# A fused attention and FFN kernel: stores split by token parity, matmuls without a reader among the first units, and PSUM copies and loads reordered

## The chip, the cores and the metric

The kernel runs on one core of a Trainium2 chip. The metric is the device time of one execution in microseconds (us). A "fast" run is one at most 1.5% above the fastest of the same kernel; all comparisons below are between fast runs. The span in a profile is 1.8 to 1.9 us shorter than the measured time of the same execution, because it reaches from the first to the last instruction only.

## The reference

```python
# attention with decay, in blocks of 64 tokens; q, k, v are (4, 8, 768, 64), lam is (8,)
for b in range(nb):
    intra = (q_b @ k_b.T * Dmask) @ v_b
    inter = (q_b * lam_pow) @ kv_state
    out_b = intra + inter
    kv_state = lam_block * kv_state + (k_b * rev_pow).T @ v_b
x = out.transpose(0, 2, 1, 3).reshape(3072, 512)
# FFN: w_in is 512 x 2048, w_out is 2048 x 512
h = x @ w_in
g = h + sin(alpha * h)**2 / alpha
return g @ w_out                      # (3072, 512), float32
```

## The kernel before

In this kernel TensorE does the matrix products ("matmuls") and writes them to the buffer PSUM; the other tiles lie in the buffer SBUF; inputs and outputs lie in HBM, the main memory. In the listings `QT` is a transposed copy of q or k, `okv` the output of a unit in PSUM, `xt` its copy in SBUF, `hps` the result of the first FFN product and `ob` an output block; a "step" of the unit loop is the time from one unit to the next.

The work is cut into 24 attention units (four of them make 512 tokens, a "group") and into FFN steps. The order in time is: units 0 to 7 (two groups); then FFN steps alone, 16 of group 0 (`hook0`) and 8 of group 1 (`hook1`); then "macros", in which a unit, FFN steps and a block of the last matrix product are woven together; then the last four output blocks.

The parts that matter here:

```python
# one 128-token output block: PSUM -> SBUF -> HBM
nc.scalar.copy(out=ob[:], in_=ops[:])
nc.sync.dma_start(out=out[r0:r0 + C, :].rearrange("(p two) d -> two p d", two=2),
                  in_=ob[:])

# one FFN step: four matmuls into hps, then
s1 = sin(alpha * hps)          # ScalarE, reads PSUM
s2 = s1 * s1                   # VectorE, GpSimd or ScalarE, by a list
gall = s2 * r + hps            # VectorE, reads PSUM and SBUF

# one of the first eight units, n
scale_q(n + 1, V); scale_k(n + 1, G)
okv = new_okv()                       # one PSUM buffer, so it waits for its last reader
intermm(n - 1, okv); outmm(n - 1, okv)
scores(n); domask(n)
kvmm(n, okv); kv_copy(n, okv); kv_decay(n, 0)
transposes(n + 1, tag, True)          # eight on TensorE, then the QT copies
outev(n - 1, okv)                     # the xt copy: last reader of okv; ScalarE
cast_v(n + 1, A)
# ... (cut)
SQ = (V, A, G, G)                     # engines of the squares, used in turn
def hook0(f):
    # ... (cut: decays, load_w_out every fourth step)
    if f == GATE:
        load(8, after=f1mm[0, f]); load(9); load(10); load(11)
def hook1(f):
    if f == 1: scale(8, G, G, A)
    if f == 3: transposes(8, "s0"); scale(9, G, G, A)
alone(NFC, hook0, (V, A, V, G))       # 16 steps of group 0
alone(NPRE, hook1)                    # 8 steps of group 1, with SQ
```

V is VectorE, A is ScalarE, G is GpSimd.

## Time and profile before

253.46 us, the median of three runs (252.28 to 255.07); the profiled execution took 254.61 us.

| stretch of the profile | us | what bounds it |
|---|---|---|
| 0 to 37.50 | 37.5 | units 0 to 7: a loop over TensorE and ScalarE, with TensorE at half clock (sixteen score matmuls take 0.64 us, later 0.42) |
| 37.50 to 73.14 | 35.6 | FFN steps alone, then the first macro |
| 73.14 to 237.96 | 164.8 | macros and last blocks: TensorE, over 97% busy |
| 237.96 to 252.83 | 14.9 | no engine works |

First the end. This is the table of busy time by stretch for the kernel before: the stretch in us from the start, its length, each engine's busy us and instructions, the granted TensorE clock, the mean busy share of the 16 DMA engines, and GB/s.

```profile
223.00:238.00 15.00, 13.92 (x63) 6.17 (x63) 0.75 (x1) 2.61 (x5) 0.00 (x0) 1.00 0.13 45
238.00:242.00 4.00, 0.00 (x0) 0.00 (x0) 0.00 (x0) 0.00 (x0) 0.00 (x0) 0.80 0.13 51
242.00:247.00 5.00, 0.00 (x0) 0.00 (x0) 0.00 (x0) 0.00 (x0) 0.00 (x0) 0.50 0.13 51
```

From 238 us on every engine's column is zero, and the DMA share stands at 0.13. That is not a lightly loaded DMA: the share is a mean over 16 engines, and 2 of them fully busy make 0.125. The trace's packet records agree: from 242 to 250 us exactly two packets are under way at any moment. Each store raises its semaphore three times, once 0.93 to 1.15 us after the issue and twice when the data land (7.71 and 7.90 us after it for the store of 216.38 us, which did not queue). So stores of 256 KB go at 51 GB/s, 5.1 us each, while the last blocks are finished every 3.45 us. A queue of stores builds up, and the kernel ends when it has drained.

Now the loop of the first units, in the timeline of the kernel before (start in us, duration in us, engine, source line, operation, count, and in brackets the idle time before and what ended it). L294 are the inter-chunk matmuls, L215 the score matmuls, L193 the transposes, L197 the QT copy, L320 the xt copy.

```profile
22.18 0.37 PE L294 MATMUL okv<-QT,kvbd_495 128*128 128x128 bf16 x2 [0.99 <-ACT xt L320]
22.48 0.64 PE L309 MATMUL okv<-ST,VB 64*64 64x128 bf16 x16
22.91 0.64 PE L215 MATMUL sp<-QT 64*64 64x128 bf16 x16
23.34 0.42 PE L243 MATMUL okv<-VB,KD 64*64 64x64 bf16 x16
...
24.10 0.63 PE L193 MATMUL pt<-iden,KD 128*128 128x128 bf16 x4
...
24.81 0.59 ACT L197 COPY QT<-pt 128x512 bf16<-128x512 bf16 x1 [0.62 <-PE pt L193]
...
25.30 0.59 ACT L320 CAST xt<-okv 128x512 bf16<-128x512 f32 x1
...
25.94 0.37 PE L294 MATMUL okv<-QT,kvbd_581 128*128 128x128 bf16 x2 [1.21 <-ACT xt L320]
```

A unit takes 25.94 - 22.18 = 3.76 us. Its last link is the xt copy, which ScalarE starts only after the QT copy, which waits for the transposes; then TensorE has idled for 1.21 us.

The clock of TensorE can't be read from the page here. Its clock row shows full speed for this stretch, but the durations do not: sixteen score matmuls take 0.64 us here and 0.42 us after 65 us. It is plainest in the weight loads of the first FFN matmuls (PEld; one precedes each matmul of 512 columns):

```profile
37.93 0.15 PEld L338 LDWEIGHTS <-w_in_sb 128*128 128x128 bf16 x1 [0.28 <-issue]
38.35 0.15 PEld L338 LDWEIGHTS <-w_in_sb 128*128 128x128 bf16 x1 [0.28 <-issue]
38.78 0.15 PEld L338 LDWEIGHTS <-w_in_sb 128*128 128x128 bf16 x1 [0.27 <-issue]
```

They come every 0.427 us, twice the 0.216 us of later ones. The trace's first clock record of this run is of 42.4 us, 4.9 us after the first FFN matmul, and the spacing halves there; before the first record the row has nothing to show and prints full speed.

### The profile page before, as it was taken

To read this page: it belongs to the slowest core of one execution; us is meant where nothing else is said; L and a number is where in the kernel's file an instruction comes from. 1 tells how busy PE (TensorE), PEld (TensorE's weight loads), DVE (VectorE), ACT (ScalarE), POOL (GpSimd) and SP (SyncE) were. 2 spreads that over 40 slices of the span, in tenths; PEclk is the share of its full clock that TensorE was granted. 3 is DMA by queue.
4 is the path that set the end of the run, shared out by engine and by line. 5 is a ranking of instruction groups with operands and counts; after the bars stand their busy time and mean duration, and the time that the engine had idled before them with its cause. 6 is when DMAs were issued, how large, how long until landed. Compare 5 with 4: busy or idle time off the path is not lost.

```text
span 252.8 us, 5265 instructions
## 1 busy us (share of the span) xinstructions
PE 213.1 (84%) x2106; PEld 113.7 (45%) x2129; DVE 152.4 (60%) x260; ACT 130.8 (52%) x214; POOL 118.5 (47%) x184
## 2 busy tenths in 40 slices
PE   0867759976899999999999999999999999989500
PEld 0546543433355554555455545454554444434200
DVE  3667534898576665686669666876686667630000
ACT  2454545967766665656565656565655444520100
POOL 5665861989569998855683366236110000000000
PEclk9999999999999999999999999999999999999955
DMA  6999596599944544444533453201010111111110
GB/s 165 292 287 256 85 157 100 99 250 225 286 108 150 161 132 150 148 130 124 155 113 104 133 155 113 83 32 41 25 30 34 40 33 36 37 38 51 51 51 37
DMA packets 45560, 29.71 MB, mean 117 GB/s; under 512 B 1488, under 2 KB 42464, under 8 KB 45536
## 3 DMA queue, kind: packets, MB, share of 16 engines
q1 hardware_dynamic: 41280, 25.17, 35.0%
q0 software_dynamic: 4224, 4.19, 10.6%
q8 instruction: 16, 0.26, 0.4%
q14 instruction: 8, 0.07, 0.1%
q10 hardware_dynamic: 32, 0.01, 0.0%
HBM read 27.28 MB, written 6.29 MB: 133 GB/s over the span
## 4 chain that ended last, share of the span: by engine, by line
PE 75%; ACT 6%; POOL 5%; DVE 3%; issue 3%; DMA 1%; ACTq 0%; POOLq 0%
PE ops L365 33%; PE hps L338 27%; PE pt L193 6%; PE sp L215 3%; PE okv L309 3%; PE okv L294 3%; ACT xt L320 2%; DVE gall L352 2%; ACT QT L197 2%; PE okv L243 1%; DMA lam_bc<-in_lam_dram 1%; POOL KD L166 1%; ACT ob L372 1%; POOL E L123 1%; POOL s_944 L351 1%
## 5 line engine op out<-in xcount | busy, mean ns | idle before, releaser
L338 PE MATMUL hps<-xt,w_in_sb 128*128 128x512 bf16 x364 | 96.1, 387 | 5.4 <-DVE gall L352 2.5
L365 PE MATMUL ops<-w_out_sb,gall 128*128 128x512 bf16 x381 | 94.6, 379 | 0.9 <-ACT ob L372 0.7
L338 PEld LDWEIGHTS <-w_in_sb 128*128 128x128 bf16 x384 | 36.8, 99 | 48.2 <-issue 9.0
L365 PEld LDWEIGHTS <-gall 128*128 128x128 bf16 x384 | 36.9, 98 | 42.6 <-issue 1.0
L226 DVE TENSOR_TENSOR ST<-sp,mask 128x512 bf16<-128x512 f32 x48 | 30.8, 684 | 10.4 <-PE sp L215 10.4
L166 POOL TENSOR_TENSOR KD<-st_k,R 128x512 bf16<-128x512 f32 x24 | 26.9, 1121 | 3.5 <-DMA st_k<-in_k_dram 3.0
L200 ACT COPY QT<-pt 128x1024 bf16<-128x1024 bf16 x16 | 16.2, 1012 | 22.8 <-PE pt L193 22.8
L372 ACT COPY ob<-ops 128x512 f32<-128x512 f32 x24 | 14.1, 586 | 19.1 <-PE ops L365 19.1
L193 PE MATMUL pt<-iden,QL 128*128 128x128 bf16 x96 | 11.1, 248 | 8.8 <-DVE QL L157 6.6
L320 ACT CAST xt<-okv 128x512 bf16<-128x512 f32 x24 | 14.1, 588 | 6.4 <-PE okv L243 5.1
L157 POOL TENSOR_TENSOR QL<-st_q,E 128x512 bf16<-128x512 f32 x16 | 17.4, 1088 | 0.0
L193 PEld LDWEIGHTS <-QL 128*128 128x128 bf16 x96 | 7.7, 109 | 13.3 <-DVE QL L157 6.6
L215 PE MATMUL sp<-QT 64*64 64x128 bf16 x384 | 11.8, 252 | 0.7 <-ACT QT L197 0.7
L309 PE MATMUL okv<-ST,VB 64*64 64x128 bf16 x384 | 11.4, 248 | 0.0
L193 PE MATMUL pt<-iden,KD 128*128 128x128 bf16 x96 | 11.2, 250 | 0.3 <-POOL KD L166 0.3
L175 ACT CAST VB<-st_v 128x512 bf16<-128x512 f32 x14 | 8.7, 621 | 4.8 <-DMA st_v<-in_v_dram 4.8
L215 PEld LDWEIGHTS <-QT 64*64 64x64 bf16 x384 | 8.0, 127 | 2.9 <-ACT QT L197 0.9
L309 PEld LDWEIGHTS <-VB 64*64 64x64 bf16 x384 | 7.7, 123 | 1.7 <-issue 1.6
L193 PEld LDWEIGHTS <-KD 128*128 128x128 bf16 x96 | 7.6, 113 | 1.0 <-POOL KD L166 1.0
L243 PE MATMUL okv<-VB,KD 64*64 64x64 bf16 x320 | 8.1, 212 | 0.0
L197 ACT COPY QT<-pt 128x512 bf16<-128x512 bf16 x8 | 4.7, 586 | 5.6 <-PE pt L193 5.6
L243 PEld LDWEIGHTS <-KD 64*64 64x64 bf16 x320 | 6.9, 130 | 0.0
(528 smaller groups left out, 307.0 us busy)
## 6 DMA issues: line engine op xcount, KB each, us to landing
st_q<-in_q_dram SPq DMA_DIRECT2D x24, 256.0 KB
st_k<-in_k_dram SPq DMA_DIRECT2D x24, 256.0 KB
st_v<-in_v_dram SPq DMA_DIRECT2D x24, 256.0 KB
out_dram<-ob SPq DMA_DIRECT2D x24, 256.0 KB
w_in_sb<-in_moe_w_in_dram POOLq DMA_DIRECT2D x4, 512.0 KB, 6.3
w_out_sb<-in_moe_w_out_dram POOLq DMA_DIRECT2D x4, 512.0 KB, 9.1
lam_bc<-in_lam_dram SPq DMA_DIRECT2D x1, 4.0 KB
alpha_r<-in_moe_alpha_dram ACTq DMA_DIRECT2D x1, 8.0 KB
```

The source lines that it names most:

```text
L157: eng.tensor_tensor(out=QL[:], in0=stage[u][0][:].rearrange("p h two e -> p two h e"), in1=E[:, :, hs].unsqueeze(3).to_broadcast([P, 2, HH ...
L166: eng.tensor_tensor(out=KD[:], in0=stage[u][1][:].rearrange("p h two e -> p two h e"), in1=R[:, :, hs].unsqueeze(3).to_broadcast([P, 2, HH ...
L193: nc.tensor.transpose(out=pts[j][:, hp, par, :], in_=cast[u, key][:, par, 2 * hp:2 * hp + 2, :], identity=iden[:])
L200: nc.scalar.copy(out=QT[:], in_=pt[:])
L215: nc.tensor.matmul(out=sp[hd][half[c], par, hp, :], lhsT=QT[half[hd], 1, hp, par, half[c]], rhs=QT[half[hd], 0, hp, :, half[c]], start=Tru ...
L226: nc.vector.tensor_tensor(out=ST[:, hd], in0=sp[hd][:], in1=mask[:].unsqueeze(2).to_broadcast([P, 2, 2, P]), op=ALU.mult)
L243: nc.tensor.matmul(out=okv[half[hd], c, 2 * P + hp * D:2 * P + (hp + 1) * D], lhsT=KD[half[c], par, h, :], rhs=VB[half[c], par, h, :], sta ...
L309: nc.tensor.matmul(out=okv[half[hd], c, hp * P:(hp + 1) * P], lhsT=VB[half[c], par, 2 * hp + hd, :], rhs=ST[half[c], hd, par, hp, :], star ...
L320: nc.scalar.copy(out=xt[g][:, 2 * hh:2 * hh + 2, bb, :, :].rearrange("p hp c i -> p c hp i"), in_=okv[:, :, 0:2 * P].rearrange("p c (hp i) ...
L338: f1mm[g, f] = nc.tensor.matmul(out=hps, lhsT=w_in_sb[:, c, f * P:(f + 1) * P], rhs=xt[g][:, c].rearrange("p b c i -> p (b c i)"), start=( ...
L365: f2mm[:] = [nc.tensor.matmul(out=ops[:], lhsT=gall[g][:, f, m * P:(m + 1) * P], rhs=w_out_sb[:, f, :], start=(f == 0), stop=(f == NFC - 1))]
L372: nc.scalar.copy(out=ob[:], in_=ops[:])
```

## The change

The change aims at all three places: the store is to use more than two DMA engines; TensorE is to be kept at full clock from the start by matmuls of zeros that nobody reads, 28 at once and four behind each unit; the xt copy goes ahead of the transposes' QT copy; in the FFN-alone steps, squares and later loads are redistributed. The diff, cut to its core:

```diff
+    N0 = 28
+    NB = 4
+    zeros = consts.tile([P, 2 * P], BF16, name="zeros")
+    nc.vector.memset(zeros[:], 0.0)
...
-            nc.sync.dma_start(out=out[r0:r0 + C, :].rearrange("(p two) d -> two p d", two=2),
-                              in_=ob[:])
+            rows = out[r0:r0 + C, :].rearrange("(p two) d -> two p d", two=2)
+            for par in range(2):
+                nc.sync.dma_start(out=rows[par], in_=ob[par * D:(par + 1) * D, :])
...
+    def busy(k):
+        if k:
+            bz = ps.tile([P, 2 * P], FP32, name="bz", tag="ops", bufs=1)
+            for _ in range(k):
+                nc.tensor.matmul(out=bz[:], lhsT=zeros[:, :P], rhs=zeros[:], start=True, stop=True)
...
-            if nxt:
-                transposes(n + 1, tag, True)
             if n > 0:
                 outev(n - 1, okv)
             if nxt:
+                transposes(n + 1, tag, True)
                 cast_v(n + 1, A)
+            busy(NB)
+    busy(N0)
     scale(0, V, G, A)
...
-    SQ = (V, A, G, G)
+    SQ = (V, A, G, V, V, A, G, V)
...
         if f == GATE:
             load(8, after=f1mm[0, f])
-            load(9); load(10); load(11)        # three lines in the kernel
...
         if f == 1:
             scale(8, G, G, A)
-        if f == 3:
+        if f == 2:
+            load(9, after=f1mm[1, f]); load(10)      # two lines
+        if f == 4:
             transposes(8, "s0")
+        if f == NPRE - 1:
+            load(11, after=f1mm[1, f])
             scale(9, G, G, A)
-    alone(NFC, hook0, (V, A, V, G))
+    alone(NFC, hook0, (V, A, V, A, G, A, V, G))
```

More of the change, by code (lines that the diff above doesn't have):

```diff
@@ L463, in alone @@
                 tag = "hps"
-            run(ffn1(g, f, sq[f % 4], tag))
+            run(ffn1(g, f, sq[f % 8], tag))
             if hook:
@@ L509, in hook0 @@
             load(8, after=f1mm[0, f])
-            load(9)
-            load(10)
-            load(11)
     def hook1(f):
@@ L516, in hook1 @@
             scale(8, G, G, A)
-        if f == 3:
+        if f == 2:
+            load(9, after=f1mm[1, f])
+            load(10)
+        if f == 4:
             transposes(8, "s0")
+        if f == NPRE - 1:
+            load(11, after=f1mm[1, f])
             scale(9, G, G, A)
-    alone(NFC, hook0, (V, A, V, G))
+    alone(NFC, hook0, (V, A, V, A, G, A, V, G))
     alone(NPRE, hook1)
```

## The prediction

> **What bounds the kernel now** (busy time by stretch, chain of waits, timeline).
>
> 1. 0 to 37.5 us: eight attention units, a step every 3.76 us (inter-chunk matmuls at 14.67, 18.43, 22.18), although loads land 2.7 us a unit apart and end at 26.2 us. Inter-chunk matmuls wait 7.0 us in six waits for the xt copy, which stands on ScalarE behind the QT copy, which waits for the transposes. TensorE is slow there: sixteen score matmuls take 0.64 us, later 0.42; the first FFN matmuls go every 0.43 us, from 43 us on every 0.215. [...]
> 2. 70 to 237 us: TensorE, warm, over 97% busy.
> 3. 238.0 to 252.8 us: no engine works. The DMA share is 0.13 at 51 GB/s: two of 16 engines. The last five stores (256 KB, 5.1 us each at this rate) come every 3.45 us and queue; the last is issued at 238.0, and the end waits for it.
>
> **What the change does.**
> - Store: its outermost dimension is 2. [...] An unqueued store now takes 7.8 us from issue to landing, 5.1 of them data[...]. Cost: a second issue, 0.5 us. The last landing moves from 251.5 to about 241.5 us: minus 10, all critical.
> - Matmuls without a reader: 28 before the first transposes, in 6 us in which TensorE waits for data; at half clock they end 0.4 us late at worst. Four more a unit, 0.4 us warm. They should warm the array by about 6 us.
> - xt copy before the QT copy: takes 1 us a unit out of the loop. With both, a unit costs about 2.7 us, bounded by loads, VectorE (2.4 us) and GpSimd (2.1 to 2.6, plus 0.9 for each weight-load issue). The FFN starts at about 31.7 instead of 37.5 us: minus 5.8.
> - FFN alone: warm from the first matmul, minus 2 us. One square in eight goes from VectorE to ScalarE in sixteen steps; two of GpSimd's four (1.04 us each) go to VectorE (0.43) in the next eight, where the chain runs over GpSimd and a 2.4 us gap for a late load. Later loads leave the DMA to the weights. Minus 1.5 us.
> - The middle stays.
>
> Sum: 10 + 5.8 + 2 + 1.5, rounded down for interference: 253.5 to about 235 us.
>
> **Chances.** Faster by over 2%: 0.96; within 2%: 0.03; slower: 0.01. Range 229 to 241.
>
> **What would show it.** End within 5 us of the last output copy; stores landing about 3 us after issue. Sixteen score matmuls of the first units 0.42 us; unit steps 2.6 to 2.9 us; first FFN matmul at 31 to 33 us, spacing 0.215; the first score matmuls after the FFN-alone stretch at 56 to 57 instead of 65.2 us; then the same macro steps of 6.65 and 8.38 us.
>
> **What would make it wrong.** The clock drops again between units (TensorE is half busy there): then the four matmuls cost 0.85 us a unit, steps stay near 3.4 us, and I get about 240. Weights landing after the earlier FFN start. If the store still used few engines, 244.

The sum came to 19.3 us and was rounded down to 18.5; that 64 rows would use more engines than two was an expectation. The costs of the extra matmuls are estimates from the spacings of 0.43 and 0.215 us of the 512-column matmuls, halved for 256 columns; that the matmuls would bring the full clock was an expectation. "Half busy" is 21.04 of 30.50 us in the profile, from 7 to 37.5 us.

## The result, and the profile after

236.21 us, the median of four runs (234.88 to 236.43), against 253.8 us for the kernel before in the same rounds. The ratio is 0.9298, with a 95% interval of 0.9235 to 0.9361. (A ratio is the mean time of one kernel's fast runs over that of the other's of the same rounds, so it is not quite the ratio of the medians quoted.)

| stretch, by the two profiles | before | after | difference |
|---|---|---|---|
| start to the first FFN matmul | 37.50 | 31.84 | -5.66 |
| 16 FFN steps alone | 16.70 | 13.62 | -3.08 |
| 8 more, to the first score matmul of unit 8 | 10.98 | 12.89 | +1.91 |
| on to the first output copy | 7.96 | 7.12 | -0.84 |
| on to the end of the last output copy | 164.82 | 164.82 | 0.00 |
| on to the end | 14.87 | 4.22 | -10.65 |
| sum | 252.83 | 234.51 | -18.32 |

One caution on the first row: in the profile before, TensorE had no full-clock period before 42.4 us. In two other profiles with the old unit loop (the store alone, and neither the order nor the extra matmuls, both below) it had one by chance, and the first FFN matmul came at 35.9 to 36.0 us. So some executions of the kernel before are probably about 1.5 us shorter than the one in the table, which fits that the medians differ by 17.6 us and the two profiles by 18.3.

(The boundary after 16 steps is taken at the 65th FFN weight load, because weight loads are complete in the trace; they run a little ahead of the matmuls.)

The end, in the table of busy time by stretch for the kernel after:

```profile
215.60:230.30 14.70, 13.92 (x63) 6.17 (x63) 0.48 (x1) 2.34 (x5) 0.00 (x0) 1.00 0.33 72
230.30:231.50 1.20, 0.00 (x0) 0.00 (x0) 0.00 (x0) 0.00 (x0) 0.00 (x0) 1.00 0.05 12
231.50:233.00 1.50, 0.00 (x0) 0.00 (x0) 0.00 (x0) 0.00 (x0) 0.00 (x0) 1.00 0.75 165
```

The last store is a short burst at a high DMA share instead of a long stretch at 0.13: the trace has 15 packets under way in the mean from 231.8 to 232.6 us, and up to 17 at once. Each half now raises its semaphore 16 times. In the page's table of DMA issues, the last number is the median time from issue to landing:

```profile
out_dram<-ob SPq DMA_DIRECT2D x48, 128.0 KB, 2.4
```

The loop of the first units, in the timeline of the kernel after (L298 inter-chunk, L219 scores, L197 transposes, L201 the QT copy, L324 the xt copy, L419 the matmuls without a reader):

```profile
13.40 0.28 PE L298 MATMUL okv<-QT,kvbd_366 128*128 128x128 bf16 x2
13.61 0.42 PE L313 MATMUL okv<-ST,VB 64*64 64x128 bf16 x16
13.86 0.39 PE L219 MATMUL sp<-QT 64*64 64x128 bf16 x16
14.32 0.32 PE L247 MATMUL okv<-VB,KD 64*64 64x64 bf16 x16
...
14.96 0.59 ACT L324 CAST xt<-okv 128x512 bf16<-128x512 f32 x1
15.41 0.40 PE L197 MATMUL pt<-iden,KD 128*128 128x128 bf16 x4 [0.44 <-POOL KD L170]
15.65 0.60 PE L419 MATMUL bz<-zeros 128*128 128x256 bf16 x4
15.89 0.58 ACT L201 COPY QT<-pt 128x512 bf16<-128x512 bf16 x1 [0.34 <-ACT xt L324]
16.08 0.27 PE L298 MATMUL okv<-QT,kvbd_454 128*128 128x128 bf16 x2
```

This step takes 2.68 us, the score matmuls 0.39 us, and the inter-chunk matmuls no longer wait for the xt copy, which is now done before the transposes. The steps from 10.69 to 28.59 us are 2.98 us in the mean. What the loop often waits for now, among the waits of this stretch (total us, times, longest), is the loads:

```profile
POOL KD L170 <- DMA st_k<-in_k_dram: 5.1, 6, 1.5
```

And the FFN starts at full clock. The line below holds 62 recorded matmuls in 14.00 us; the first are spaced 0.216 us.

```profile
31.84 14.00 PE L342 MATMUL hps<-xt,w_in_sb 128*128 128x512 bf16 x62 [0.16 <-issue]
```

The one stretch that became longer is around 50 us. The timeline of the kernel after there:

```profile
48.77 3.40 DVE L355 TENSOR_TENSOR s_1127<-s_1125 128x512 bf16<-128x512 bf16 x1
48.84 1.06 POOL L161 TENSOR_TENSOR QL<-st_q,E 128x512 bf16<-128x512 f32 x1
49.85 1.04 POOL L170 TENSOR_TENSOR KD<-st_k,R 128x512 bf16<-128x512 f32 x1
50.85 1.03 POOL L355 TENSOR_TENSOR s_1153<-s_1151 128x512 bf16<-128x512 bf16 x1
...
52.21 0.75 DVE L356 SCALAR_TENSOR_TENSOR gall<-s_1127,r_sb,hps 128x512 bf16<-128x512 bf16 x1
...
53.66 0.59 PE L197 MATMUL pt<-iden,QL 128*128 128x128 bf16 x4 [2.90 <-DVE gall L356]
...
54.90 0.15 PEld L342 LDWEIGHTS <-w_in_sb 128*128 128x128 bf16 x1 [0.28 <-issue]
55.32 0.15 PEld L342 LDWEIGHTS <-w_in_sb 128*128 128x128 bf16 x1 [0.27 <-issue]
```

A square on VectorE, which takes 0.42 us where no GpSimd operation overlaps it (50 of the 82 of this profile), is there for 3.40 us: it ends 0.29 us after the last of three GpSimd operations without a gap (48.84 to 51.88 us). The `gall` behind it frees a PSUM buffer late, TensorE idles for 2.90 us, and then the weight loads are 0.42 us apart: the clock has fallen to half for one period of 3.41 us (53.47 to 56.88 us in the trace's clock records).

### The profile page after: what moved, and what is told of

It is laid out like the page before. It is cut to its first block, busy times and chain, and to the rows that moved or that the text cites. A ratio compares the mean times of both kernels' runs of the same rounds, so it can differ in the third digit from the quotient of the medians.

```text
span 234.5 us, 5410 instructions
## 1 busy us (share of the span) xinstructions
PE 213.9 (91%) x2166; PEld 113.9 (49%) x2189; DVE 154.4 (66%) x261; ACT 131.6 (56%) x216; POOL 115.5 (49%) x182
## 4 chain that ended last, share of the span: by engine, by line
PE 71%; SPq 7%; DVE 6%; POOL 4%; issue 4%; ACT 4%; DMA 2%; POOLq 0%; ACTq 0%
PE ops L369 35%; PE hps L342 26%; SPq L81 7%; PE pt L197 3%; PE sp L219 2%; DMA st_k<-in_k_dram 2%; DVE gall L356 2%; PE okv L313 2%; PE okv L298 2%; DVE s_1127 L355 1%; DVE QL L161 1%; ACT xt L324 1%; PE okv L247 1%; ACT ob L376 1%; POOL KD L170 1%
## 5 line engine op out<-in xcount | busy, mean ns | idle before, releaser
L342 PE MATMUL hps<-xt,w_in_sb 128*128 128x512 bf16 x364 | 94.8, 383 | 3.1 <-ACT xt L324 1.2
L324 ACT CAST xt<-okv 128x512 bf16<-128x512 f32 x24 | 14.1, 587 | 6.1 <-PE okv L247 5.2
L161 POOL TENSOR_TENSOR QL<-st_q,E 128x512 bf16<-128x512 f32 x16 | 17.4, 1088 | 0.0
L197 PE MATMUL pt<-iden,QL 128*128 128x128 bf16 x96 | 9.6, 223 | 4.8 <-DVE gall L356 2.9
L197 PE MATMUL pt<-iden,KD 128*128 128x128 bf16 x96 | 9.6, 224 | 3.5 <-POOL KD L170 3.4
L197 PEld LDWEIGHTS <-QL 128*128 128x128 bf16 x96 | 6.8, 99 | 9.7 <-issue 4.1
L419 PE MATMUL bz<-zeros 128*128 128x256 bf16 x60 | 10.3, 326 | 1.1 <-DVE warm L95 1.1
L219 PE MATMUL sp<-QT 64*64 64x128 bf16 x384 | 9.9, 221 | 0.7 <-ACT QT L201 0.7
L313 PE MATMUL okv<-ST,VB 64*64 64x128 bf16 x384 | 9.8, 218 | 0.0
L197 PEld LDWEIGHTS <-KD 128*128 128x128 bf16 x96 | 6.3, 100 | 4.7 <-POOL KD L170 4.7
L161 DVE TENSOR_TENSOR QL<-st_q,E 128x512 bf16<-128x512 f32 x8 | 7.8, 970 | 1.0 <-DMA st_q<-in_q_dram 0.9
L419 PEld LDWEIGHTS <-zeros 128*128 128x128 bf16 x60 | 6.5, 117 | 2.7 <-DVE warm L95 1.1
L219 PEld LDWEIGHTS <-QT 64*64 64x64 bf16 x384 | 6.4, 106 | 2.9 <-ACT QT L201 0.8
```

Of the source, the lines that this page charges most:

```text
L161: eng.tensor_tensor(out=QL[:], in0=stage[u][0][:].rearrange("p h two e -> p two h e"), in1=E[:, :, hs].unsqueeze(3).to_broadcast([P, 2, HH ...
L197: nc.tensor.transpose(out=pts[j][:, hp, par, :], in_=cast[u, key][:, par, 2 * hp:2 * hp + 2, :], identity=iden[:])
L219: nc.tensor.matmul(out=sp[hd][half[c], par, hp, :], lhsT=QT[half[hd], 1, hp, par, half[c]], rhs=QT[half[hd], 0, hp, :, half[c]], start=Tru ...
L324: nc.scalar.copy(out=xt[g][:, 2 * hh:2 * hh + 2, bb, :, :].rearrange("p hp c i -> p c hp i"), in_=okv[:, :, 0:2 * P].rearrange("p c (hp i) ...
L342: f1mm[g, f] = nc.tensor.matmul(out=hps, lhsT=w_in_sb[:, c, f * P:(f + 1) * P], rhs=xt[g][:, c].rearrange("p b c i -> p (b c i)"), start=( ...
L419: nc.tensor.matmul(out=bz[:], lhsT=zeros[:, :P], rhs=zeros[:], start=True, stop=True)
```

## The experiments

Eleven experiments ran (ten other kernels and the kernel after once more), all correct. Experiments on the kernel after are compared by their ratio to the kernel before.

### The store alone

The kernel before, with only the store of the change.

> The kernel before with only the store changed to two DMAs of 64 rows. My theory (16 engines carry each half instead of 2): the last landing comes about 3.5 us after the last output copy instead of 14.9, so about 243 us (minus 10.5), stores land about 2.4 us after issue as in the kernel after, and the first FFN matmul stays at 37.5 us. Rival (the gain of the store depends on the rest of the change): less than 8 us.

Measured: 243.34 us, ratio 0.9587 (0.952 to 0.9654). The profile ends 4.2 us after the last output copy. One part was missed: the first FFN matmul came at 35.93 us, not at 37.5. The trace shows why: in this execution TensorE happened to run at full clock for one period (13.13 to 16.54 us), which made one step 2.7 us long, and then fell back: from 16.6 to 36 us the granted clock was 0.50, with TensorE busy for 12.95 of 19.40 us. So about 1.6 us of this profile's gain is luck of the clock; the store gives 10.7 us at the end whatever the rest does. The rival (less than 8 us) is refuted.

### Two DMAs, but by columns

```diff
-            for par in range(2):
-                nc.sync.dma_start(out=rows[par], in_=ob[par * D:(par + 1) * D, :])
+            for half in range(2):
+                cs = slice(half * DM // 2, (half + 1) * DM // 2)
+                nc.sync.dma_start(out=rows[:, :, cs], in_=ob[:, cs])
```

> The kernel after, but the two DMAs of a block halve the columns instead of the parities: again two DMAs of 128 KB, each with an outermost dimension of 2. If the number of engines is what counts (my theory): DMA share 0.13 in the last 10 us, end 14 to 15 us or more after the last output copy, about 247 us. If it were the number or the size of the DMAs (rival): as the kernel after, 236 us.

Measured: 248.22 us, ratio 0.9772. The stretches after the last output copy of this run (230.7 us):

```profile
230.70:236.00 5.30, 0.00 (x0) 0.00 (x0) 0.00 (x0) 0.04 (x1) 0.00 (x0) 0.78 0.14 48
236.00:241.00 5.00, 0.00 (x0) 0.00 (x0) 0.00 (x0) 0.00 (x0) 0.00 (x0) 0.50 0.14 48
```

The same number of DMAs, of the same size, issued at the same places, still run at a DMA share of 0.14, as of about two engines, and the end is 16.0 us behind the copy. So it is not that there are two smaller DMAs: in these runs an outermost dimension of the pattern of 2 went with a share of 0.13 to 0.14, whole or in two DMAs, and one of 64 with the short end of 4.2 us.

### No extra matmuls

```diff
-    N0 = 28
-    NB = 4
+    N0 = 0
+    NB = 0
```

> The kernel after without any matmul that nobody reads. Theory A (the new copy order alone takes the loop down to the loads, the warm clock mostly helps the first FFN matmuls): sixteen score matmuls take 0.64 us in the units, unit steps about 2.8 to 3.0 us, first FFN matmul at 32.5 to 33.5 us, spaced 0.43 us for some 5 us, in all 238 to 239.5 us. Theory B (the warm clock makes the gain of the units): steps of 3.4 us or more, first FFN matmul after 35 us, 240 us or more.

Measured: 238.57 us, ratio 0.9391. The first FFN matmul came at 32.55 us, spaced 0.43 us for 2.3 us. Theory A holds for the total. For the score matmuls it was too simple: groups of sixteen took 0.64 us in some units and 0.39 to 0.42 in others, because the clock now rose and fell in periods of 3.4 and 6.8 us (full 14.36 to 21.18, half to 24.60, full to 28.01, half to 34.84). The faster loop alone did not hold the full clock. (The FFN matmuls were slow for 2.3 us, not for some 5.)

### Extra matmuls only at the start

```diff
-    NB = 4
+    NB = 0
```

> The kernel after with the 28 matmuls at the start, but none behind each unit. If the four of each unit keep the clock up: score matmuls go from 0.42 us back to 0.64 us per sixteen somewhere in the units, and the time rises by 1 to 3 us, near the run without any. If the units keep it up by themselves: 0.42 us throughout, and within 0.5 us of the kernel after, 236.

Measured: 238.27 us (236.79 to 239.05), ratio 0.9368, near the run without any. The clock records: full from 3.75 us, half from 10.58 to 13.99 us, and half again from 24.23 to 34.47 us. So the full clock of the start does not last by itself: with the 28 in place, the four matmuls behind each unit make nearly all of the gain. A run with these four and without the 28 was not made, so what the 28 are worth then is open.

### The old copy order

The xt copy back behind the transposes; the extra matmuls kept.

> The kernel after with the xt copy put back behind the transposes and the QT copy. If the gains of warm clock and order overlap (my theory, as the loads set a floor of 2.7 us): unit steps about 2.8 to 3.0 us, first FFN matmul at 32.3 to 33.5 us, total up by 0.5 to 1.5 us. If they add (rival: the prediction's 1 us a unit for the order alone): steps of 3.5 us, first FFN matmul at 36 us or later, up by 4 us or more.

This run, the one with the old squares and loads and the first one with the first square on ScalarE were timed in the same five rounds as the kernel after once more:

> The kernel after once more, as the yardstick of this group: 235 to 236.5 us. Is the stretched first square of the last eight FFN-alone steps (3.4 us) there in this profile too, and does the clock fall after it? I expect the stretch again, and the clock drop in most but not all executions (times between 234.9 and 236.4).

The kernel after: 235.75 us, ratio 0.9294 (0.9252 to 0.9336). The square was stretched again (3.40 us), and the clock fell behind it, in this profile for 6.83 us. Of its six runs the two with a mean granted clock of 0.998 and 0.999 took 234.8 and 234.9 us, the other four (0.980 to 0.991) 235.7 to 237.0 us. The run-to-run spread of this kernel goes with the granted clock; where it fell in the executions without a profile is not recorded.

The old order: 236.85 us, ratio 0.9344 (0.9295 to 0.9393). The total is up by 0.5%, 1.3 us, within what overlap predicted, though the two intervals overlap; but the steps were longer than I expected (3.23 us in the mean from 14.88 to 31.02 us) and the first FFN matmul came at 34.01 us, 2.2 us late, of which some was made up later because the clock did not fall at 53 us in this execution. Neither theory had the step right; the rival's total is refuted.

This profile also separates the stretched square from the drop of the clock: the square is as long as in the kernel after and TensorE idles as long, but the granted clock (the number before the DMA share in the last line, a stretch of the table of busy time) stays at 1.00.

```profile
50.95 3.40 DVE L355 TENSOR_TENSOR s<-s 128x512 bf16<-128x512 bf16 x1
55.84 0.38 PE L197 MATMUL pt<-iden,QL 128*128 128x128 bf16 x4 [2.90 <-DVE gall L356]
54.00:60.00 6.00, 4.11 (x54) 2.26 (x55) 5.33 (x9) 4.69 (x8) 0.64 (x2) 1.00 1.13 266
```

From the 65th FFN weight load to the first output copy it takes 18.8 us here, 20.0 us in the kernel after (one period of 3.41 us at half clock) and 20.6 us in its second profile (6.83 us).

### Neither the order nor the extra matmuls

> The kernel after without the matmuls that nobody reads and with the old copy order. Alone, taking away the matmuls cost 2.5 us and the order 1.1 us. If the two stand in for each other (my theory): together more than their sum, steps of 3.75 us, first FFN matmul at 36 to 37.5 us, 241 to 243 us. If they add (rival): 239 to 239.8 us.

Measured: 242.45 us, ratio 0.9545 (0.9498 to 0.9592). In units of a kernel before of 254 us, neither is 242.4, the order alone (the run without extra matmuls) 238.5, the extra matmuls alone (the run with the old order) 237.3, and both 236.1. The order alone gains 3.9 us, the matmuls alone 5.1, both together 6.3 and not 9.0 (each of the four times is uncertain by some 1 to 1.4 us). They shorten the same loop, and the loads set a floor; the order alone comes down to it (six steps of 3.0 us in the mean, as with both), the matmuls alone to 3.3 us. The first FFN matmul was at 35.97 us, just below the range I gave, again with one lucky full-clock period.

### The old squares and loads

The lists of squares, the gates of the loads, and the places of the second scaling and of the transposes as in the kernel before.

> The kernel after with the squares, the gates of the later loads and the places of the second scale and of the transposes as before. The prediction gave this part 1.5 us: then 237.5 us. If the stretched square on VectorE (3.4 us against 0.42) spends that gain: within 0.7 us of the kernel after.

Measured: 236.17 us (235.68 to 238.74), ratio 0.934 (0.9288 to 0.9392), against 0.9294 for the kernel after: no clear difference. Its profile shows a gain and a loss that cancel. Old against new: the 16 steps take 14.74 against 13.62 us (the new way gains 1.12), the next stretch 10.98 against 12.89 (it loses 1.91), the rest up to the first output copy 7.74 against 7.12 (it gains 0.62). There is no square over 1.5 us in this profile and no drop of the clock. The first square of the last eight is on VectorE here too, but it starts late in a GpSimd operation with only one more behind it, and takes 1.46 us.

### The first square of the last eight on ScalarE

```diff
-    SQ = (V, A, G, V, V, A, G, V)
+    SQ = (A, A, G, V, V, A, G, V)
```

> The kernel after with one square moved: the first of the last eight FFN-alone steps goes to ScalarE (0.63 us) instead of VectorE. Theory (VectorE waits there for GpSimd's chain of three operations[...]): no square over 1.3 us, no TensorE gap of 2.9 us at 51 us, no half clock after it, and 232 to 233.5 us, minus 2.5 to 4. Rival (the late thing is a load or a weight chunk): the gap stays in another place and the time changes by less than 1 us.

Measured: 233.35 us (232.93 to 233.95), ratio 0.9202 (0.9164 to 0.9239), clear of the kernel after in the same rounds. No square of the FFN-alone steps is stretched; the stretch of the last eight steps is 8.49 us instead of 12.89, of which the following stretch gives back 1.9 (9.03 instead of 7.12 us): ScalarE there waits 2.9 us for the load of v of unit 9. The best of the versions that were tried is this one, level with the next two.

### q of unit 8 scaled on VectorE

```diff
-            scale(8, G, G, A)
+            scale(8, V, G, A)
```

> The kernel after with the first of GpSimd's three back-to-back operations (the scaling of q of unit 8) given to VectorE; the stretched square stays on VectorE. Theory (the square waits out GpSimd's unbroken chain): GpSimd now has one operation there and then a gap, so the square takes 1.1 to 1.6 us instead of 3.40, the TensorE gap behind it shrinks from 2.9 us to about 1, and the total falls by 1 to 3 us. Rival (the square waits for the weight DMA's traffic or for its own input): 3.4 us as in the kernel after, the same time.

Measured: 233.78 us, ratio 0.9208 (0.9163 to 0.9253). The timeline of this run, the same square:

```profile
48.76 1.42 DVE L355 TENSOR_TENSOR s<-s 128x512 bf16<-128x512 bf16 x1
48.83 1.05 POOL L170 TENSOR_TENSOR KD<-st_k,R 128x512 bf16<-128x512 f32 x1
...
50.67 1.04 POOL L355 TENSOR_TENSOR s<-s 128x512 bf16<-128x512 bf16 x1 [0.79 <-ACT s L349]
```

The square starts at the same time as in the kernel after, behind the same weight DMA, and ends 0.30 us after GpSimd's unbroken run, now of one operation (in the kernel after: 0.29 us after a run of three). The gap of TensorE behind it is 1.56 us, down from 2.90 but not to the expected 1. The rival (the weight DMA's traffic, or the square's own input) is refuted. By the recorded starts the square came first, by 0.07 us, in both runs; in the kernel after the square at 46.76 us, 0.06 us ahead of a GpSimd operation, took 0.42 us all the same. So the runs show that the square can last as long as GpSimd's unbroken run; which of the two has to wait, and when, they do not show. The `gall` operation, which has one input in PSUM, took 0.74 to 0.75 us beside GpSimd work and without it (all 96 in the kernel after, 37 of them with at least 0.2 us of overlap).

### The first square on ScalarE, and unit 9 loaded earlier

```diff
         if f == GATE:
             load(8, after=f1mm[0, f])
+            load(9)
...
         if f == 2:
-            load(9, after=f1mm[1, f])
-            load(10)
+            load(10, after=f1mm[1, f])
```

(and the edit of the list of squares above)

> The run with the first square on ScalarE, and the load of unit 9 issued together with that of unit 8. In that run ScalarE waits 2.9 us for v of unit 9 at 55.7 us. If this load is what ends that stretch now: the wait is gone, the first output copy comes 1 to 2 us earlier than at 63.2 us, and 231.5 to 232.5 us in all. Rival (the load only takes the DMA from the weights, as the change feared): no gain, or a wait for a weight chunk.

Measured: 233.68 us, ratio 0.9189 (0.9146 to 0.9232): no gain that the interval can show over 0.9202. The wait for unit 9 is gone, but ScalarE now waits just as long for unit 10:

```profile
60.97 0.62 ACT L179 CAST VB<-st_v 128x512 bf16<-128x512 f32 x1 [2.92 <-DMA st_v<-in_v_dram]
```

This profile also started the FFN 0.6 us later; both profiles have a drop of the clock for one period in the units (at 19.2 us here, at 19.9 us in the other), so that does not explain it. From there to the first output copy it is 0.75 us shorter. So my theory of that load was too narrow: the wait moved one unit on. Whether loading all of them earlier would pay is open.

## Why the prediction was right

The total was right: 235.0 was predicted, 236.21 measured, within the range of 229 to 241.

- **The store: minus 10, and it was 10.65.** The DMA share of 0.13 named the number of engines, and the expectation that 64 rows would use more of them, not shown by any trace before, held both ways: outermost dimension 64 gave 16 semaphore updates, up to 17 packets under way at once and a store of 2.4 us; outermost dimension 2 stayed at a share of 0.14 even in two DMAs. Nothing but the drain depended on it: the middle is 164.82 us in both profiles.
- **The first units: minus 5.8, and it was 5.66.** The unit loop fell from 3.76 to 2.98 us in the mean (2.6 to 2.9 was predicted), and it waits for loads. That both the order and the clock were each worth most of this alone was not in the prediction; it counted them together, and that was right only because it put the floor of 2.7 us under their sum. That 5.66 lands so close to 5.8 owes something to luck: both numbers start from the same profile, one without a full-clock period in the units.
- **Full clock by about 6 us: 5.68.** The fear that the clock falls between units did not come true in the profile of the kernel after, and in the run with the 28 matmuls only at the start, without the four per unit, it did. The four are no guarantee: in two later profiles with the same unit loop (both with the first square on ScalarE) the clock fell for one period, at 19.9 and 19.2 us.
- **The FFN alone: minus 2 for the full clock, which was right, and minus 1.5 for the squares and loads, the term that was mis-sized.** From the first FFN matmul to the first output copy the gain was 2.0 us (3.08 - 1.91 + 0.84), not 3.5. The profile with the old squares and loads splits it: from the first FFN matmul to the first output copy the kernel before takes 35.6 us, that run, at full clock, 33.5, and the kernel after 33.6. So the clock gave 2.2 us and the new squares and loads nothing. The prediction costed a square on VectorE at 0.43 us, its time when no GpSimd operation overlaps it (0.416 to 0.427 us in the profile before). The change leaves the first square of the last eight on VectorE and puts it where GpSimd begins a chain of three operations, and it was there for 3.40 us; TensorE idled for 2.90 us and then ran at half clock. The first score matmul of unit 8 came at 58.35 us instead of the predicted 56 to 57. The terms of the prediction add up to 19.3 us and were rounded down to 18.5 "for interference"; no interference was named, so that this covered half of the loss is luck.
- **Later loads leave the DMA to the weights.** Nothing in the runs shows a gain of this: the median time from issue to landing of a w_in chunk is 6.3 us before and 6.5 after, and opening one load earlier cost nothing that can be measured. No run undid the later loads alone.

What the drop of the clock costs is read from single profiles. From the 65th FFN weight load to the first output copy, the run with the old order (stretched square, no drop) takes 18.8 us, the two profiles of the kernel after (stretched square and drop) 20.0 and 20.6, and the runs without the stretched square 17.5 (first square on ScalarE) and 17.4 (q on VectorE). So the square costs some 1.3 us and the drop some 1.2 to 1.8 us more. The idle time of TensorE before it is 2.90 us with and without the drop; why the clock fell in one and not in the other is open.

## What to carry to other kernels

Read the DMA share in a stretch where only one kind of DMA runs: here 0.13, two sixteenths, at 51 GB/s came with an outermost dimension of 2 in the pattern, and splitting that dimension off into separate DMAs was the remedy (share 0.75 from 231.5 to 233 us). Judge TensorE's clock from the durations of equal matmuls: in the kernel before the clock row showed full speed up to its first record at 42.4 us, while weight loads were 0.427 us apart. Where the clock is half, a few matmuls without a reader in idle places can be worth more than they cost (here some 2.4 us, by the ratios with and without them), but then check in several profiles that the clock holds (in two later ones it fell for one period). And when work moves to VectorE, look at what GpSimd does at that moment: here a square on VectorE lasted as long as GpSimd's whole chain (3.40 us instead of 0.42).
